# Transposed row maxima in the unused columns of the score banks, a third bank for products, a spread-out norm, Wo split during attention

## The chip, the cores and the metric

One NeuronCore of a Trainium2 chip runs the whole kernel. The metric is the device time of one execution in microseconds (us), the median of a few runs. In the profile the engines are PE (matrix multiply), PEld (its weight loads), DVE (vector), ACT (scalar), POOL (GpSimd) and SP (which issues most DMAs). PSUM, where PE writes its results, has eight banks of 2 KB per partition.

## The reference

Four layers on x of 2048 rows by 640 columns: a Fourier layer, an attention layer, and both again with the same weights.

```python
x = A_x
x = x + _A_ref(_layernorm(x), dft_seq_re, dft_seq_im, dft_hid_re, dft_hid_im)
x = x + _B_ref(_layernorm(x), wqkv, wo)
# ... and the same two lines once more
# _A_ref: a = x @ hid_re.T; b = x @ hid_im.T; y = seq_re @ a - seq_im @ b
# _B_ref: 32 heads of width 20, window 256 (key j is seen by query i where 0 <= i-j < 256):
#   scores = q @ k.T * 20**-0.5; p = softmax(masked scores); out = (p @ v) @ wo
```

## The kernel before

Every product of two fp32 matrices is made of fp16 halves (high and low part), so each 128x128 block costs three matmuls. `spectral(layer, ...)` is a Fourier layer and `attention(layer, ...)` an attention layer; they run as spectral 0, attention 0, spectral 1, attention 1.

**Order.** In the spectral layers a scheduler sets each engine's order at build time from priorities; generators in the list `side` advance one step at each `tick()`, of which there are seven per inner round `j`. In attention (`in_turn[0]` is true) each PE instruction is tied behind the one before it, so PE's order is the order in which the code issues it. All engines work strictly in the order of their own streams.

**Attention.** Rows are taken in 8 blocks `b` of 256, heads in 16 pairs; a step `g` handles one tile of 128 rows for one pair of heads, 256 steps per layer. In step `g` stand, in this order: `scores(g)` (four matmuls into the PSUM tile `sp` of two banks, of whose 512 columns per bank 384 are used; then DVE masks with COPY_PREDICATED, L1025, and takes the row maxima `m` with TENSOR_REDUCE, L1029); `by_key(g-7)` (the same scores transposed, tile `tp`, which need the maxima; ACT makes probabilities of them, L1068); every fourth step `values` and `back` (probabilities times v); then `run_fill`, which adds as many matmuls of other work as the step has time for. That other work (projections of the next block, output products, transpositions) is written to the PSUM tile `pf`, one bank each, from a pool of two; `new_f()` gives the next. It is emptied by ACT and DVE (`early`, L327 and L328; `x`, L869).

Every fourth step ends with `hand_on(n)`, which hands the maxima of four steps to `by_key`: ACT and DVE split them into `tops` (L1035, L1036), PE transposes `tops` in four matmuls into the tile `hp` (a bank of its own, pool `ph`), and two copies bring the result into rows of the query stack `qs`: ACT the rows of the first head (L1047), DVE those of the second (L1045, which waits for ACT's). `scores(g+1)` is what PE has next behind it. In the first block `qs` is a tile named `ks` in the profile.

PSUM's eight banks in attention: `pf` 2, `sp` 2, `tp` 2, `pv` 1, `hp` 1.

**The last round of a spectral layer.** From round `j` = 1 on, `finish(0)` and then `finish(1)` read the first four finished row tiles back from DRAM (`x2d`), normalise them on DVE (`norm_steps`, tiles `lnst`, `lnt`, `lny`), split them (`xs`) and transpose them on PE into `early`. `finish`'s second argument `pace` says how many norm steps go into one tick: 2 for the first call, 1 for the second.

**Wo.** In spectral 0, `b_split(0, 20)` scales and splits the weights of attention: 15 chunks of wqkv go back to DRAM (`bwd`), 5 chunks of wo stay in SBUF (`bo`), one chunk per five ticks. In attention, `slow_step()` advances the first generator of the list `slow` by one step per `g`.

Of the kernel before, what the change touches and what calls it, by code (L numbers as in the profile page):

```python
# [11 lines left out]
F32 = mybir.dt.float32  # L12
F16 = mybir.dt.float16
I32 = mybir.dt.int32
AF = mybir.ActivationFunctionType
OP = mybir.AluOpType
AX = mybir.AxisListType

S, D, H, DH, P = 2048, 640, 32, 20, 128
NT = S // P  # L20
ND = D // P
# [17 lines left out]
NEXT_STEPS = (10, 22)  # L39
# [19 lines left out]
def body(ctx: ExitStack, tc: tile.TileContext, x_in, cmat, whid, wqkv, wo, out):  # L59
    nc = tc.nc  # L60
# [45 lines left out]
    in_turn, latest = [False], [None]  # L106
# [72 lines left out]
    def new_f():  # L179
        return pf_.tile([P, 512], F32, tag="f", name="pf", bufs=2)  # L180
# [112 lines left out]
    class Projections:  # L293


        def __init__(self):
            n = 3 * ND * D
            big = new_big()
            self.w = [big[:, k * n:(k + 1) * n].rearrange("p (a b) -> p a b", a=ND) for k in range(2)]
            load_behind([(big[:, k * n:(k + 1) * n], bw_d[k].rearrange("p a b -> p (a b)")) for k in range(2)])  # L300
            self.rows = {}
            self.turn = 0
            self.stack = {}

        def new_rows(self, b):
            t = new_early()
# [3 lines left out]
            self.rows[b] = (x, [st[:, k] for k in range(NST)])  # L310

        def qk(self, b, w, ct):
            pf = new_f()
            cols = slice(w * D + ct * P, w * D + (ct + 1) * P)
            xt, stores = self.rows[b]
            k = 0
            for dt in range(ND):
                for l, r in ((0, 0), (0, 1), (1, 0)):
                    matmul(pf[:, :QB], self.w[l][:, dt, cols], xt[:, :, r, dt, :],
                                     start=k == 0, stop=k == 14)  # L320
                    k += 1
                    if k < 15:
                        yield 109
            t = stores[self.turn % len(stores)]
            self.turn += 1
            down = 8.0 / (X_UP * W_UP)
            nc.scalar.activation(t[:, 0], pf[:, :QB], AF.Copy, scale=down)  # L327
            nc.vector.scalar_tensor_tensor(t[:, 1], pf[:, :QB], down, t[:, 0], op0=OP.mult, op1=OP.subtract)  # L328
            load(qk_d[b][w].rearrange("a (c p) t -> c p a t", p=P)[ct], t)
            yield 109  # L330
# [5 lines left out]
    def spectral(layer, res_src, hidden, first):  # L336
        with ExitStack() as st:
# [204 lines left out]
            def main_c(r, j):  # L542
                res, cc, y, zb = state.pop((r, j))
                x0, x1 = res
                z = product(r, zb, cc, 6, False, True)
                add(x0[:, hi], z, x0[:, hi])
                tick()
                z = product(r, y, cc, 5, False, True)
                add(x1[:, lo], z, x1[:, lo])
                last = r == NR - 1  # L550
                for k in range(2):
                    nc.scalar.dma_start((x2_d if last else acc_d)[2 * j + k], res[k])
                if last and j == 0:
                    side.append(chain(finish(0, 2), finish(1, 1)))
                tick()

            def ahead(proj):
# [11 lines left out]
            def finish(j, pace):  # L569
                xs = [sb.tile([P, D], F32, tag="xin", name="x2", bufs=NXIN) for k in range(2)]  # L570
                for k in range(2):
                    load(xs[k], x2_d[2 * j + k])
                yield 1
                ys, xss = [], []
                for k, _ in enumerate(norm_steps(xs, ys)):
                    if k % pace == 0:
                        yield 1
                for y in ys:
                    xs = keep.tile([P, 2, D], F16, tag="xs", name="xs", bufs=2)
                    split(xs[:, 0], xs[:, 1], y, nc.gpsimd)  # L580
                    xss.append(xs)
                    yield 1
                proj.new_rows(j)
                for k, xs in enumerate(xss):
                    for m in range(2):
                        transposed(xs, m, proj.rows[j][0][:, k])
                        yield 1
                    finished[0] += 1
# [51 lines left out]
            def b_split(n0, n1):  # L640
                fs = {n: b_chunk(n) for n in range(n0, n0 + 3)}
                for _ in range(4):
                    yield 1
                for n in range(n0, n1):
                    f = fs.pop(n)
                    if n < 15:
                        t = keep.tile([P, 2, D], F16, tag="xto", name="bst", bufs=2)
                        hi, lo, sc = t[:, 0], t[:, 1], wsc[:, 0:1]
                    else:
                        hi, lo, sc = bo[0][:, n - 15], bo[1][:, n - 15], wsc[:, 1:2]  # L650
                    nc.scalar.activation(hi, f, AF.Copy, scale=sc)
                    yield 1
                    nc.vector.scalar_tensor_tensor(lo, f, sc, hi, op0=OP.mult, op1=OP.subtract)
                    if n < 15:
                        cs = slice((n % 3) * D, (n % 3 + 1) * D)
                        for k in range(2):
                            nc.scalar.dma_start(bw_d[k][:, n // 3, cs], t[:, k])
                    if n + 3 < n1:
                        fs[n + 3] = b_chunk(n + 3)
                    for _ in range(4):  # L660
                        yield 1

            def keep_w():
# [22 lines left out]
            for r in range(NR):  # L686
# [22 lines left out]
                for j in range(NJ):  # L709
                    n = r * NJ + j  # L710
                    if first:
                        if (r, j) == (0, 1):
                            side.append(chain(keep_w(), b_max()))
                        if (r, j) == (1, 0):
                            side.append(chain(b_scale(), b_split(0, 20)))
                    if r == NR - 1 and j == 3:
                        early_qk = ahead(proj)
                        side.append(early_qk)
# [41 lines left out]
    def attention(layer, proj, dst, final):  # L760
        with ExitStack() as st:
# [3 lines left out]
            def banks(name):  # L765
                return pool(name, space=bass.MemoryType.PSUM)
# [5 lines left out]
            else:  # L772
                pv_ = banks("pv")
                ps = banks("ps")
            ph = banks("ph")

            in_turn[0] = True
            VS_ = {}
# [115 lines left out]
            def next_norm(i, x3):  # L894
# [6 lines left out]
                if i < NT - 1:  # L901
                    fill.extend(Unit(now[0] + TURN_STEPS, g, "turn", now[0], [], True) for g in live[-1])

            def rows_norm(b, x2s):

                ys = []
                yield from norm_steps(x2s, ys)
                for t, y in enumerate(ys):
                    xs = new_xs()
                    split(xs[:, 0], xs[:, 1], y, nc.gpsimd)  # L910
                    live[-1].extend(rows_turn(b, xs, t, k) for k in range(2))
                    fill.extend(Unit(now[0] + TURN_STEPS // 2, g, ("rows", b), now[0], [], True) for g in live[-1])
                    yield
# [86 lines left out]

            TOP, PT, topped = {}, {}, [None]

            def place(g):

                b, r = divmod(g, 2 * NP)
                return 2 * b + r // 2 % 2, 2 * (r // 4) + r % 2

            def scores(g):
# [1 line left out]
                b = i // 2  # L1010
                qs = QS[b]
                t0 = (i % 2) * P
                sp = ps.tile([P, 2, 512], F32, tag="s", name="sp")
                if i % 2 == 0:
                    parts = [(0, 2 * P, b - 1, 0), (2 * P, 3 * P, b, 0)]
                else:
# [14 lines left out]
            def hand_on(n):  # L1031

                b, q = divmod(n, NP // 2)
                m, hl = TOP.pop(n), tops[n % 2]
                nc.scalar.activation(hl[:, :, :, 0], m, AF.Copy, scale=-1.0 / M_UP)  # L1035
                nc.vector.scalar_tensor_tensor(hl[:, :, :, 1], m, -1.0 / M_UP, hl[:, :, :, 0], op0=OP.mult, op1=OP.subtract)  # L1036
                hp = ph.tile([P, 4, P], F16, name="hp")
                for k in range(4):
                    transpose(hp[:66, k], hl[:, k].rearrange("p a b -> p (a b)")[:, :66], idh)
                for pi in range(2):  # L1040
                    rs = slice(64 * pi, 64 * pi + 2)
                    o = QS[b][rs, 2 * q:2 * q + 2].rearrange("r p (i t) -> r i p t", i=2)
                    t = hp[rs].rearrange("r (i p) t -> r i p t", i=2)
                    if pi:
                        nc.vector.tensor_copy(o, t)  # L1045
                    else:
                        nc.scalar.activation(o, t, AF.Copy)  # L1047
# [117 lines left out]
            total = NBQ * 60 * 136 + (NBQ - 1) * (150 * 109 + 60 * 136 + (4 if final else 8) * ND * 56)  # L1165
            total += 0 if final else 120 * 136
            total += (NBQ - 2) * 4 * ND * 56 - FIRST_FILL
            for g in range(NS):
                now[0] = g
                b, r = divmod(g, 2 * NP)  # L1170
# [10 lines left out]
                if g < NG and r == VALUE_LAG:  # L1181
# [7 lines left out]
                    if b == NBQ - 1 and not final:  # L1189
                        hidden = Hidden(xu_d)  # L1190
                        hidden.load()
                        for k in range(2):
                            hidden.fetch(k)
                            fill.append(Unit(g + NEXT_STEPS[k], hidden.stage(k, None), "next", NG + k))
                slow_step()
                n, m = divmod(g - VALUE_LAG, 4)
                if m == 0 and 0 <= n < NG // 4:
# [54 lines left out]
```

## Time and profile before

| | |
|---|---|
| median of 3 runs | 2322.34 us (2322.32 to 2322.77) |
| profiled execution, time | 2325.37 us |
| profiled execution, span from first to last instruction | 2323.6 us |
| busy, share of the span | PE 92%, DVE 75%, ACT 52%, POOL 52% |
| mean granted TensorE clock | 0.982 of full speed |
| first scores of attention 0 | 607.2 us |
| last scores of the kernel | 2293.9 us |

Busy PE is the sum of its matmuls' durations; what is left of 100% is time in which no matmul ran. A row of the waits says which instruction of an engine waited for which of another: total us, number of waits, longest. In the order of a program below, `[waits X_49]` names the engine whose count of finished instructions the instruction waits for, not the instruction.

### The profile page before, as it was taken

What the parts mean: (1) busy time and instruction counts of PE and PEld (TensorE: products, weight loads), DVE (VectorE), ACT (ScalarE), POOL (GpSimd) and SP (SyncE); (2) the same over time, 40 slices, a digit from 0 to 9 for tenths busy, and PEclk for the clock granted to TensorE, in tenths of its full rate; (3) what the DMA queues carried; (4) which work ended last, traced back from release to release, by engine and by line L of the source; (5) the groups of instructions that cost most, each with busy time, mean ns of one, the idle gap of its engine ahead of it and who ended that gap; (6) DMA issues with size and microseconds to landing.
All of it is one profiled execution on the core that took longest, in us unless ns stands there. A gap on an engine that the chain in (4) does not pass through costs nothing.

```text
span 2323.6 us, 54624 instructions
## 1 busy us (share of the span) xinstructions
PE 2143.3 (92%) x21985; PEld 1503.6 (65%) x21985; DVE 1746.8 (75%) x3761; ACT 1210.8 (52%) x2120; POOL 1199.3 (52%) x1453
## 2 busy tenths in 40 slices
PE   7999899989898999999889999999898989999997
PEld 5667566657566666666556777777665666666664
DVE  7887969767678788887767857584768777777674
ACT  5334444333266666676654344334325666666665
POOL 6776757655234444443347868584552334434343
PEclk9999999999999999999999999999999999999999
DMA  5864746454332332233324535464542322232120
GB/s 185 293 208 150 244 151 203 138 209 136 105 86 51 99 86 72 61 93 88 139 88 146 199 124 186 139 204 158 187 145 71 87 58 66 70 93 72 51 77 24
DMA packets 187602, 292.92 MB, mean 126 GB/s; under 512 B 13908, under 2 KB 120660, under 8 KB 178004
## 3 DMA queue, kind: packets, MB, share of 16 engines
q1 hardware_dynamic: 157108, 223.55, 31.7%
q10 hardware_dynamic: 30240, 65.88, 7.6%
q8 instruction: 172, 2.82, 0.5%
q14 instruction: 82, 0.67, 0.1%
HBM read 202.51 MB, written 86.87 MB: 125 GB/s over the span
## 4 chain that ended last, share of the span: by engine, by line
PE 63%; DVE 25%; DMA 5%; issue 3%; ACT 3%; POOL 1%; SPq 0%; DVEq 0%; ACTq 0%; POOLq 0%
PE pf L112 22%; PE y L112 11%; PE z L112 7%; PE x L112 7%; PE pv L112 7%; DVE m L1029 6%; PE sp L112 4%; DVE sp L1025 4%; DVE cc L480 4%; PE tp L112 2%; DVE qs L1045 1%; DMA x<-x2d 1%; DVE lnst L125 1%; DVE early L328 1%; DMA x2d<-res 1%
## 5 line engine op out<-in xcount | busy, mean ns | idle before, releaser
L112 PEld LDWEIGHTS <-cc 128*128 128x128 f16 x5376 | 530.5, 99 | 244.4 <-issue 33.1
L1068 ACT ACTIVATE ptq<-tp,shift,alpha 128x768 f32<-128x768 f32 (+2 forms) x512 | 484.4, 946 | 190.0 <-PE tp L112 145.9
L112 PEld LDWEIGHTS <-big 128*128 128x128 f16 x4320 | 409.1, 98 | 141.9 <-issue 32.1
L1073 POOL TENSOR_SCALAR_AFFINE_SELECT ptq<-ptq 128x512 f32<-128x512 f32 x224 | 144.2, 644 | 507.3 <-ACT ptq L1068 506.9
L1029 DVE TENSOR_REDUCE m<-sp 128x2 f32<-128x512 f32 (+1 forms) x512 | 344.9, 674 | 15.6
L112 PE MATMUL pf<-early,big 128*128 128x256 f16 x2400 | 310.1, 274 | 1.5 <-DVE early L328 1.4
L1025 DVE COPY_PREDICATED sp<-mask,sp 128x256 f32<-128x256 int32 x448 | 190.6, 425 | 129.1 <-PE sp L112 118.8
L112 PE MATMUL y<-zc,cc 128*128 128x320 f16 x1728 | 269.9, 304 | 16.0 <-DVE pf L503 16.0
L477 ACT ACTIVATE cc<-cs 128x512 f16<-128x512 f32 x256 | 152.3, 623 | 250.3 <-POOL cs L470 104.6
L112 PE MATMUL pf<-big 128*128 128x320 f16 x1680 | 241.9, 302 | 11.0 <-DVE zc L250 5.1
L480 DVE SCALAR_TENSOR_TENSOR cc<-cs,cc 128x512 f16<-128x512 f32 x256 | 231.4, 921 | 3.6 <-ACT cc L477 3.6
L1075 POOL TENSOR_SCALAR_AFFINE_SELECT ptq<-ptq 128x512 f32<-128x512 f32 x256 | 164.9, 644 | 94.4 <-ACT ptq L1068 94.4
L480 DVE SCALAR_TENSOR_TENSOR cc<-cq,cc 128x512 f16<-128x512 f32 x192 | 202.1, 1053 | 0.0
L112 PE MATMUL sp<-ks,qs 62*128 62x256 f16 (+1 forms) x1792 | 154.2, 249 | 45.0 <-DVE m L1029 39.8
L112 PE MATMUL pv<-ptq,v 128*32 128x128 f32 (+1 forms) x3840 | 186.9, 334 | 0.0
L112 PE MATMUL z<-zc,cc 128*128 128x320 f16 x1152 | 181.0, 302 | 4.2 <-DVE res L503 4.0
L112 PE MATMUL x<-zc,cc 128*128 128x320 f16 x1152 | 182.0, 302 | 0.0
L112 PE MATMUL pf<-big,early 128*128 128x320 f16 x960 | 158.3, 301 | 0.4 <-DVE early L927 0.4
L112 PE MATMUL tp<-qs,ks 62*128 62x128 f16 x2688 | 150.8, 217 | 3.2 <-ACT ptq L1068 2.9
L112 PE MATMUL pf<-bo,ot 128*128 128x320 f16 x840 | 145.6, 303 | 3.0 <-DVE x L869 1.1
L112 PEld LDWEIGHTS pv<-ptq,v 128*32 128x32 f32 x3840 | 108.3, 111 | 57.7 <-issue 4.0
L112 PEld LDWEIGHTS <-ks 62*128 62x128 f16 x3008 | 116.0, 95 | 39.8 <-DVE m L1029 23.2
(142 smaller groups left out, 3382.6 us busy)
## 6 DMA issues: line engine op xcount, KB each, us to landing
cq<-in_cmat_dram SPq DMA_DIRECT2D x64, 1024.0 KB
accd<-res ACTq DMA_DIRECT2D x96, 320.0 KB
res<-accd SPq DMA_DIRECT2D x96, 320.0 KB
x<-x2d SPq DMA_DIRECT2D x64, 320.0 KB
qkd<-early SPq DMA_DIRECT2D x160, 128.0 KB
ks<-qkd SPq DMA_DIRECT2D x108, 160.0 KB
qs<-qkd SPq DMA_DIRECT2D x84, 160.0 KB
x2d<-res ACTq DMA_DIRECT2D x32, 320.0 KB
```

What stands on the lines that cost most here:

```text
L112: i = getattr(nc.tensor, what)(*args, **kw)
L125: nc.vector.bn_stats(st[:, h], x[:, h * 320:(h + 1) * 320])
L328: nc.vector.scalar_tensor_tensor(t[:, 1], pf[:, :QB], down, t[:, 0], op0=OP.mult, op1=OP.subtract)
L477: nc.scalar.activation(cc[m][:, 0], f, AF.Copy, scale=C_UP)
L480: nc.vector.scalar_tensor_tensor(cc[m][:, 1], f, C_UP, cc[m][:, 0], op0=OP.mult, op1=OP.subtract)
L1025: nc.vector.copy_predicated(sp[:, :, 2 * P:3 * P], mask[:, None, :].to_broadcast([P, 2, P]), far)
L1029: topped[0] = nc.vector.tensor_reduce(TOP[g // 4][:, g % 4], sp[:, :, c0:3 * P], axis=AX.X, op=OP.max).ins
L1045: nc.vector.tensor_copy(o, t)
L1068: nc.scalar.activation(q[:, h:h + 2, a0 + first:a0 + 3], tp[:, :, first * P:3 * P].rearrange("p a (b c) -> p a b c", c=P), AF.Sigmoid, bia ...
L1073: nc.gpsimd.affine_select(out=q[:, :, a0], in_=q[:, :, a0], pattern=[[0, 4], [-1, P]], base=0, channel_multiplier=1, compare_op=OP.is_gt, ...
L1075: ins = nc.gpsimd.affine_select(out=q[:, :, a0 + 2], in_=q[:, :, a0 + 2], pattern=[[0, 4], [1, P]], base=0, channel_multiplier=-1, compare ...
```

## The change

1. The tile `sp` is made once per attention layer and not once per step, and the bank of `hp` is given up: PE's four transpositions go into columns 384 to 511 of the two `sp` banks, which the scores leave unused (`hp[0]`, `hp[1]`), and the two copies read from there.
2. The bank that is free becomes the pool `p3`: in attention every third `new_f()` comes from it, so `pf` products rotate over three banks.
3. `finish` yields three times behind its loads (one before), and every norm step has its own tick in both calls (`pace` 1, and `pace` now counts ticks per step).
4. `b_split` ends at chunk 15 and takes six ticks per chunk. `split_wo()` does the five chunks of wo as the first generator of `slow` in attention 0: it loads them on SP's queue into `res` buffers and splits one per step on ACT and DVE.

```diff
@@ class Projections
+            self.new_f = new_f
...
-            pf = new_f()
+            pf = self.new_f()
@@ spectral
-                    side.append(chain(finish(0, 2), finish(1, 1)))
+                    side.append(chain(finish(0, 1), finish(1, 1)))
...
-                yield 1
+                for _ in range(3):
+                    yield 1
                 ys, xss = [], []
-                for k, _ in enumerate(norm_steps(xs, ys)):
-                    if k % pace == 0:
+                for _ in norm_steps(xs, ys):
+                    for _ in range(pace):
                         yield 1
...
-                            side.append(chain(b_scale(), b_split(0, 20)))
+                            side.append(chain(b_scale(), b_split(0, 15)))
@@ attention
-            ph = banks("ph")
+            p3 = banks("p3")
+            third = [0]
+
+            def new_f():
+                third[0] += 1
+                if third[0] % 3 or not in_turn[0]:
+                    return pf_.tile([P, 512], F32, tag="f", name="pf", bufs=2)
+                return p3.tile([P, 512], F32, tag="f", name="pf")
+
+            proj.new_f = new_f
...
+            def split_wo():
+                fs = [keep.tile([P, D], F32, tag="res", name="wst", bufs=4) for n in range(2)]
+                for n in range(2):
+                    load(fs[n], wo[:, n])
+                yield
+                for n in range(ND):
+                    f, sc = fs.pop(0), wsc[:, 1:2]
+                    nc.scalar.activation(bo[0][:, n], f, AF.Copy, scale=sc)
+                    nc.vector.scalar_tensor_tensor(bo[1][:, n], f, sc, bo[0][:, n], op0=OP.mult, op1=OP.subtract)
+                    if n + 2 < ND:
+                        fs.append(keep.tile([P, D], F32, tag="res", name="wst", bufs=4))
+                        load(fs[-1], wo[:, n + 2])
+                    yield
...
+            sp = ps.tile([P, 2, 512], F32, tag="s", name="sp")
+            hp = [sp[:, k, 3 * P:].bitcast(F16).rearrange("p (a b) -> p a b", a=2) for k in range(2)]
...
             def scores(g):
-                sp = ps.tile([P, 2, 512], F32, tag="s", name="sp")
...
             def hand_on(n):
-                hp = ph.tile([P, 4, P], F16, name="hp")
                 for k in range(4):
-                    transpose(hp[:66, k], hl[:, k].rearrange("p a b -> p (a b)")[:, :66], idh)
+                    transpose(hp[k // 2][:66, k % 2], hl[:, k].rearrange("p a b -> p (a b)")[:, :66], idh)
                 for pi in range(2):
                     rs = slice(64 * pi, 64 * pi + 2)
                     o = QS[b][rs, 2 * q:2 * q + 2].rearrange("r p (i t) -> r i p t", i=2)
-                    t = hp[rs].rearrange("r (i p) t -> r i p t", i=2)
+                    t = sp[rs, :, 3 * P:].bitcast(F16).rearrange("r i (p t) -> r i p t", p=2)
...
+            if layer == 0:
+                slow.append(split_wo())
```

What the programs' orders say, at three places.

PE at a hand-over (`hand_on`, then the next `scores`; here `tops_77` is the buffer with the split maxima), before:

```order
L112 MATMUL hp<-idh,tops_77 66x128
L112 LDWEIGHTS tops_77
L112 MATMUL hp<-idh,tops_77 66x128
L112 LDWEIGHTS qs [waits DVE_49]
L112 MATMUL sp<-ks,qs 128x128 [waits PE_49]
L112 LDWEIGHTS qs
L112 MATMUL sp<-ks,qs 128x128
```

and after the change:

```order
L112 LDWEIGHTS tops_77
L112 MATMUL sp<-idh,tops_77 66x128 [waits DVE_49]
L112 LDWEIGHTS tops_77
L112 MATMUL sp<-idh,tops_77 66x128
L112 LDWEIGHTS qs
L112 MATMUL sp<-ks,qs 128x128 [waits DVE_49]
L112 LDWEIGHTS qs
L112 MATMUL sp<-ks,qs 128x128
```

No instruction moved, but the waits did. Before, the weight load ahead of the next scores waited for a DVE count that is reached with the row maxima of the step before (L1029). Now the first score matmul waits for a DVE count that is reached with the DVE copy out of the same banks (L1069, before L1045), in all 126 hand-overs that have scores behind them (63 in each layer); and the first transposition waits for the last row maxima taken from `sp`.

DVE around that copy (in the same hand-over's neighbourhood, attention 0), before:

```order
L1025 COPY_PREDICATED sp<-mask,sp 128x2x128 [waits DVE_49,PE_49]
L1029 TENSOR_REDUCE m<-sp 128x2 [waits DVE_49]
L1045 COPY qs<-hp 2x2x2x128 [waits Activation_49]
L1116 RECIPROCAL r<-pv 128x8 [waits PE_49]
L1117 TENSOR_TENSOR o<-pv,r 128x160 [waits DVE_49,Pool_49]
```

and after the change:

```order
L950 COPY xto<-pf 128x640 [waits PE_49]
L1069 COPY qs<-sp 2x2x2x128 [waits Activation_49]
L1050 COPY_PREDICATED sp<-mask,sp 128x2x128 [waits DVE_49,PE_49]
L1054 TENSOR_REDUCE m<-sp 128x2 [waits DVE_49]
L1140 RECIPROCAL r<-pv 128x8 [waits PE_49]
```

The copy of the maxima, which stood behind the mask of the next scores (and here behind their maxima too), now stands ahead of it.

DVE in the last round of spectral 0, where `finish(0)` ends (`lny` are the two normalised tiles, `lnt` the last norm steps, `cc` splits of the Fourier matrix, `pf<-y` and `res<-z` the sums that empty PE's banks), before:

```order
L142 TENSOR_TENSOR lnt<-lnt 128x2 [waits DVE_49]
L143 SCALAR_TENSOR_TENSOR lnt<-lnt 128x2 [waits DVE_49]
L147 TENSOR_SCALAR lny<-x_5744,lnmv,lnt 128x640 [waits DVE_49]
L147 TENSOR_SCALAR lny<-x_5745,lnmv,lnt 128x640
L503 SCALAR_TENSOR_TENSOR pf<-y,pf 128x320 [waits PE_49]
L480 SCALAR_TENSOR_TENSOR cc<-cs,cc 128x512 [waits Activation_49] x2
L390 COPY early<-pf 128x640 [waits PE_49] x2
```

and after the change:

```order
L143 SCALAR_TENSOR_TENSOR lnt<-lnt 128x2 [waits DVE_49]
L504 SCALAR_TENSOR_TENSOR pf<-y,pf 128x320 [waits PE_49]
L481 SCALAR_TENSOR_TENSOR cc<-cs,cc 128x512 [waits Activation_49]
L147 TENSOR_SCALAR lny<-x_5724,lnmv,lnt 128x640 [waits DVE_49]
L481 SCALAR_TENSOR_TENSOR cc<-cs,cc 128x512 [waits Activation_49]
L147 TENSOR_SCALAR lny<-x_5725,lnmv,lnt 128x640
L504 SCALAR_TENSOR_TENSOR res<-z,res 128x320 [waits PE_49,Pool_49]
```

The sum `pf<-y` now stands ahead of the normalised tiles, and on PE the first transposition of them stands 40 matmuls later than before (58 in spectral 1).

More of the change, by code (lines that the diff above doesn't have):

```diff
@@ L645, in b_split @@
                     f = fs.pop(n)
[L646 to L650, printed above, removed]
+                    t = keep.tile([P, 2, D], F16, tag="xto", name="bst", bufs=2)
+                    hi, lo, sc = t[:, 0], t[:, 1], wsc[:, 0:1]
                     nc.scalar.activation(hi, f, AF.Copy, scale=sc)
@@ L653, in b_split @@
                     nc.vector.scalar_tensor_tensor(lo, f, sc, hi, op0=OP.mult, op1=OP.subtract)
[L654 to L657, printed above, removed]
+                    cs = slice((n % 3) * D, (n % 3 + 1) * D)
+                    for k in range(2):
+                        nc.scalar.dma_start(bw_d[k][:, n // 3, cs], t[:, k])
                     if n + 3 < n1:
                         fs[n + 3] = b_chunk(n + 3)
-                    for _ in range(4):
+                    for _ in range(5):
                         yield 1
@@ L1193, in attention @@
                             hidden.fetch(k)
-                            fill.append(Unit(g + NEXT_STEPS[k], hidden.stage(k, None), "next", NG + k))
+                            fill.append(Unit(g + NEXT_STEPS[k], hidden.stage(k, None, new_f), "next", NG + k))
                 slow_step()
```

## The prediction

> **What bounds the kernel now.** I read first the busy time by stage (spectral 0, attention 0, spectral 1, attention 1; columns: window, its length, busy time of each engine, clock, DMA share, GB/s), then PE's waits, then single hand-overs in the timeline.
>
> ```profile
> core 0: us, PE busy (x) PEld busy (x) DVE busy (x) ACT busy (x) POOL busy (x), PEclk, DMA share, GB/s
> 0.00:607.00 607.00, 551.32 (x4014) 391.89 (x4015) 474.68 (x881) 248.06 (x482) 385.71 (x326) 0.97 0.57 190
> 607.00:1243.00 636.00, 580.44 (x7421) 400.03 (x7421) 499.50 (x1302) 409.86 (x676) 263.22 (x450) 0.99 0.29 84
> 1243.00:1738.00 495.00, 482.35 (x3573) 348.99 (x3571) 346.72 (x551) 184.48 (x370) 333.42 (x272) 0.99 0.51 171
> 1738.00:2323.60 585.60, 529.15 (x6979) 362.74 (x6978) 425.90 (x1029) 368.45 (x594) 216.90 (x412) 0.99 0.25 68
> ```
>
> PE is the bound everywhere: 580.4 of 636.0 us and 529.2 of 585.6 us in the two attentions. So all the time that better waits can give back there is 55.6 + 56.4 = 112 us, and any new wait of PE is added to the span. PE's longest waits over the whole span (total us, times, longest):
>
> ```profile
> PE sp L112 <- DVE m L1029: 49.9, 91, 1.8
> PE y L112 <- DVE pf L503: 25.0, 11, 5.3
> PE pf L112 <- DVE early L328: 19.6, 25, 1.6
> PE pf L112 <- DVE x L869: 12.5, 14, 4.2
> ```
>
> The first is PE waiting for the row maxima before it may overwrite `sp`; the last two are products waiting for one of the two `pf` banks. Now a hand-over in the middle of attention 0 (start, duration):
>
> ```profile
> 907.50 0.39 PE L112 MATMUL hp<-idh,tops 128*66 128x128 f16 x4
> 907.82 0.34 PE L112 MATMUL sp<-ks,qs 62*128 62x128 f16 x4
> 907.92 0.59 ACT L1047 ACTIVATE qs<-hp 2x512 f16<-2x512 f16 x1 [0.37 <-PE hp L112]
> 908.20 0.43 DVE L1025 COPY_PREDICATED sp<-mask,sp 128x256 f32<-128x256 int32 x1
> 908.66 0.42 DVE L1045 COPY qs<-hp 2x512 f16<-2x512 f16 x1
> ```
>
> PE goes from the transpositions (modelled end 907.89) straight into the next scores at 907.82, 0.07 us before that end, while ACT and DVE only begin to copy. The copies end at 909.08 and nobody on PE waits for them. That is what the change takes away.
>
> **The hand-over, step by step.** In the changed program the first score matmul behind the transpositions waits for the DVE copy. Nothing of PE's work stands between them, so PE idles from the end of the transpositions to the end of that copy. What the copy needs, in the last hand-over of the kernel, where nothing stood in its way:
>
> ```profile
> 2298.44 0.39 PE L112 MATMUL hp<-idh,tops 128*66 128x128 f16 x4
> 2298.86 0.59 ACT L1047 ACTIVATE qs<-hp 2x512 f16<-2x512 f16 x1
> 2299.48 0.42 DVE L1045 COPY qs<-hp 2x512 f16<-2x512 f16 x1 [3.36 <-ACT qs L1047]
> ```
>
> ACT starts 0.03 us behind the transpositions' end (2298.83), DVE 0.03 us behind ACT's end (2299.45), and the copy ends at 2299.90, 1.07 us behind the transpositions. From the end of a DVE instruction to PE's start it takes 0.05 us, in the wait of 2.93 us at the end of spectral 0:
>
> ```profile
> 509.03 0.48 DVE L503 SCALAR_TENSOR_TENSOR pf<-y,pf 128x320 f32<-128x320 f32 x1
> 509.56 1.79 PE L112 MATMUL y<-zc,cc 128*128 128x320 f16 x12 [2.93 <-DVE pf L503]
> 511.19 1.25 PE L112 MATMUL x<-zc,cc 128*128 128x320 f16 x8
> ```
>
> With the 0.07 us of overlap that is lost, the floor of a hand-over is 1.07 + 0.05 + 0.07 = 1.19 us. A late one, where DVE was busy with a norm:
>
> ```profile
> 1969.93 0.39 PE L112 MATMUL hp<-idh,tops 128*66 128x128 f16 x4
> 1971.48 0.41 DVE L1025 COPY_PREDICATED sp<-mask,sp 128x256 f32<-128x256 int32 x1
> 1971.92 0.42 DVE L1045 COPY qs<-hp 2x512 f16<-2x512 f16 x1
> ```
>
> Here the copy ends 2.02 us behind the transpositions, so 2.14 us in all; 0.41 us of it is the mask, which the new order puts behind the copy. How many are late, from the rows of the tile `hp` (minimum/median/maximum in ns; then the idle time that the transpositions ended):
>
> ```profile
> L1047 ACT ACTIVATE qs<-hp x112: 570/587/587, 678.2 to 2298.9; 2x512 f16<-2x512 f16 x112
> L1045 DVE COPY qs<-hp x112: 422/422/424, 678.9 to 2299.5; 2x512 f16<-2x512 f16 x112
>   PE hp L112: 56.8, 77
> ```
>
> The two copies' durations hardly vary, and in 77 of 128 hand-overs ACT sat idle for the transpositions. I take the floor for those and 0.4 us more for the other 51, nearer the floor than the late one, since the mask's 0.41 us is gone: 1.19 + 51/128 x 0.4 = 1.35 us. With scores behind it a hand-over occurs 63 times in each attention: 126 x 1.35 = **+170 us**, bounds 126 x 1.19 = 150 and 126 x 2.14 = 270. Queued behind the waiting matmul are the other scores, `by_key`'s matmuls and so ACT's probabilities; they come as much later as PE does, and DVE, in its copy, stands ahead of the next mask and maxima, so it cannot work ahead either.
>
> By the rows alone one could hope that the wait is a formality, since matmuls and copies ran side by side at 907.92 without harm, in different banks: the price would be 0. [...]
>
> **What comes back.** (a) Waits for the maxima, 49.9 us: a hand-over stands before every fourth step's scores, and its wait takes the place of about a quarter, 12; of the other 37 I take a quarter, 9, since DVE is given 1.2 us in every four steps to catch up: **-21 us** (0 to -50). (b) The third bank: 19.6 + 12.5 = 32.1 us of waits for two banks; three give a product one more product's time, over a microsecond against waits of 0.8 us on average: **-27 us** (0 to -32). (c) The spread norm. The waits around `finish` in spectral 0 (500 to 525 us) and spectral 1 (1640 to 1655 us):
>
> ```profile
> PE pf L112 <- ACT xs L159: 5.3, 1, 5.3
> PE y L112 <- DVE pf L503: 2.9, 1, 2.9
> PE pf L112 <- POOL xs L160: 1.1, 1, 1.1
> ...
> PE y L112 <- DVE pf L503: 5.3, 1, 5.3
> PE pf L112 <- ACT xs L159: 3.6, 1, 3.6
> PE pf L112 <- POOL xs L160: 0.4, 1, 0.4
> ```
>
> They sum to 18.6 us. The norm takes DVE as long as before, but PE now has 40 and 58 matmuls more to do before it needs the result, at 12 in 1.63 us (509.56 to 511.19) 5.4 and 7.9 us: at most 13.3 us come back, I take **-12 us** (0 to -19).
>
> **What is moved at no cost.** Wo's five splits leave spectral 0 for the first steps of attention 0:
>
> ```profile
> L112 PE MATMUL pf<-bo,ot x840: 296/299/474, 704.8 to 2300.8; 128*128 128x320 f16 x168
> L651 ACT ACTIVATE bo<-wst,wsc x5: 812/817/819, 352.9 to 384.0; 128x640 f16<-128x640 f32 x5
> L653 DVE SCALAR_TENSOR_TENSOR bo<-wst,wsc,bo x5: 871/1479/1883, 357.8 to 396.8; 128x640 f16<-128x640 f32 x5
> ```
>
> That is about 5 x 1.48 us of DVE and 5 x 0.82 us of ACT, from a stage where DVE is 78% busy into one where it is 79% busy: 0, and 5 x 1.48 = 7.4 us either way if neither stage covers it. The first product that reads `bo` runs at 704.8 us, 97 us behind the start of attention 0, so the five loads on SP's queue (DMA share 0.29 there), ahead of which stand only the first stacks' loads, have time; the next block's loads come behind them. The weight load ahead of the scores no longer waits itself; it takes less than the copies' wait and hides in it: 0. `b_split`'s wider spacing ends before the last round, where its result is loaded: 0.
>
> **The clock.** New idle time could lower the granted clock. Four stretches of 3.4 us, two by two in sequence (columns as in the first view):
>
> ```profile
> 661.90:665.30 3.40, 1.47 (x18) 0.93 (x16) 2.98 (x7) 2.24 (x5) 1.56 (x3) 1.00 0.00 0
> 665.30:668.70 3.40, 3.40 (x33) 1.56 (x32) 1.32 (x4) 0.97 (x3) 0.64 (x1) 0.50 0.02 5
> 712.00:715.40 3.40, 2.15 (x22) 1.48 (x23) 3.24 (x14) 1.46 (x2) 1.23 (x2) 1.00 0.04 14
> 715.70:719.10 3.40, 2.14 (x28) 1.39 (x29) 2.98 (x8) 2.54 (x4) 1.83 (x3) 1.00 0.25 96
> ```
>
> After a stretch with 1.47 us of PE work the clock was 0.50 for the next; after one with 2.15 us it stayed at 1.00. A hand-over alone leaves 3.4 - 1.35 = 2.05 us of work, just on the safe side; a second wait beside it is not. A half-clock stretch costs up to 3.4/2 = 1.7 us: I take three, **+5 us**, and 126/3 = 42 of them, 71 us, as the far end.
> [...]
>
> **Sum.** 170 - 21 - 27 - 12 + 5 = +115 us on the span of 2323.6, so 2438.6 us. The profiled execution took 2325.37 us, 3.0 above the median of 2322.34; against that median the sum is 2322.3 + 115 = **2437 us**, with own bounds of 2395 to 2495.
>
> **Rivals.** *The waits absorb it.* DVE's backlog is the cause of most waits, and PE's pauses clear it: hand-overs at their floor, 150, and all of 49.9 + 32.1 + 18.6 = 100.6 us back: +49, **2372 us**. For it: all three groups wait for DVE or ACT. Against: in its copy DVE is held back too. *The clock swings:* 71 us in place of 5, **2503 us**; the same place is reached by late hand-overs at 1.9 us each. For it: 2.05 us is close to 1.47. *The wait is over in time* (the other side): the copy is done before PE reaches the scores, and (b) and (c) remain: 2322 - 39 = **2283 us**. It decides from the point where a hand-over costs less than (21 + 27 + 12)/126 = 0.48 us; against it, the copies alone last 0.59 + 0.42 = 1.01 us, one behind the other, in all of the trace's hand-overs shown, with no other work of PE between. *The spread norm and the third bank do nothing:* +154, 2476, inside the range.
>
> **Chances.** Forecast 0.70; absorbed (2330 to 2395) 0.16; clock or late hand-overs (above 2495) 0.09; in time 0.04; and 0.01 for no change within 0.2%, about what a measurement of this kernel can tell. So slower 0.95, same 0.01, faster 0.04. The range leaves out the last two and the upper end of the third: 2380 to 2500 us.
>
> **What would show it.** In the changed profile: a row "PE sp <- DVE qs" (the copy) with about 126 waits and 150 to 180 us; PE's transpositions named `sp<-idh,tops`; `sp <- m` below 35 us; `pf <- early` and `pf <- x` below 10 us together; the waits around `finish` near 6 us; attention 0 near 690 us and attention 1 near 640; clock above 0.97. I am wrong if that row is missing or its waits average under half a microsecond, or if the clock falls below 0.95 in attention.

## The result and the profile after

The changed kernel takes 2446.49 us (2445.51 to 2447.54), 1.0534 times the kernel before, with a 95% interval of 1.0516 to 1.0552. It is slower by about 124 us; 115 had been forecast. Its profiled execution has a span of 2445.8 us, 122 us above the 2323.6 of before, and the account below is made of these two spans. The times of the experiments are compared as ratios to the kernel before on the same chip.

The stages again, cut at the same places of the program (columns as in the prediction's first view; last line the sum):

```profile
0.00:602.00 602.00, 547.22 (x4016) 390.03 (x4016) 473.66 (x876) 246.25 (x479) 385.68 (x333) 0.98 0.56 190
602.00:1300.00 698.00, 584.36 (x7410) 412.44 (x7411) 505.90 (x1306) 418.27 (x679) 263.53 (x442) 0.97 0.27 78
1300.00:1792.00 492.00, 483.85 (x3586) 349.68 (x3583) 347.77 (x551) 184.53 (x370) 333.78 (x280) 0.99 0.51 172
1792.00:2445.80 653.80, 539.97 (x6978) 378.40 (x6978) 430.28 (x1028) 375.05 (x593) 215.84 (x400) 0.97 0.22 60
sum 2445.80, PE 2155.41 PEld 1530.55 DVE 1757.60 ACT 1224.10 POOL 1198.82; mean PE 538.85 PEld 382.64 DVE 439.40 ACT 306.02 POOL 299.71
```

All of the loss is in the two attentions: 636.0 to 698.0 us and 585.6 to 653.8 us, together +130; the spectral layers became 5 and 3 us shorter. PE is busy 2155.4 us in place of 2143.3, so of the 122 us some 12 are busy time and 110 are idle time. (Busy PE in these tables is the time in which at least one matmul ran, not the sum of the matmuls' durations: matmuls that overlap count once, and an overlap that is lost adds to it.) Which idle time, from PE's waits in the changed kernel:

```profile
PE sp L112 <- DVE qs L1069: 136.9, 110, 2.8
PE sp L112 <- DVE m L1054: 37.9, 63, 1.7
...
PE sp L112 <- DVE ks L1069: 20.2, 16, 2.1
...
PE pf L112 <- DVE x L877: 5.9, 7, 1.7
...
PE pf L112 <- DVE early L329: 2.3, 3, 0.9
```

The first and the third row did not exist before: 110 + 16 = 126 waits of the scores for the copy of the transposed maxima, 157.1 us, 1.25 us each. The rows that the third bank was for fell from 32.1 to 8.2 us. One hand-over in the middle of attention 0, engine by engine:

```profile
986.27 0.39 PE L112 MATMUL sp<-idh,tops 128*66 128x128 f16 x4
986.69 0.59 ACT L1071 ACTIVATE qs<-sp 2x512 f16<-2x512 f16 x1 [0.36 <-PE sp L112]
987.31 0.42 DVE L1069 COPY qs<-sp 2x512 f16<-2x512 f16 x1 [0.81 <-ACT qs L1071]
987.79 0.34 PE L112 MATMUL sp<-ks,qs 62*128 62x128 f16 x4 [1.13 <-DVE qs L1069]
```

The reader should see a chain with one link per engine and no gap over 0.06 us in it: transpositions to 986.66, ACT to 987.28, DVE to 987.73, PE at 987.79. PE waits 1.13 us, which is the median of the 126 waits (the least is 1.13, the longest 2.84). Before, PE's next scores began 0.07 us ahead of the end of that chain's first link. That overlap is lost too: the four transpositions and the four scores took 0.66 us of PE together at 907.50 before, and take 0.39 + 0.34 = 0.73 us here. In 126 hand-overs (0.066 us each in the mean) this is some 8 us, which stand in PE's busy time and not in the waits.

### The profile page after: what moved, and what is told of

The parts are those of the page before. It is cut to its first block, busy times and chain, and to the rows that moved or that the text cites. A ratio compares the mean times of both kernels' runs of the same rounds, so it can differ in the third digit from the quotient of the medians.

```text
span 2445.8 us, 54756 instructions
## 1 busy us (share of the span) xinstructions
PE 2155.4 (88%) x21985; PEld 1530.6 (63%) x21985; DVE 1757.6 (72%) x3761; ACT 1224.1 (50%) x2120; POOL 1198.8 (49%) x1453
## 4 chain that ended last, share of the span: by engine, by line
PE 62%; DVE 22%; ACT 6%; DMA 5%; issue 4%; POOL 1%; SPq 0%; ACTq 0%; DVEq 0%; POOLq 0%
PE pf L112 25%; PE y L112 9%; PE pv L112 7%; PE sp L112 6%; PE x L112 6%; PE z L112 6%; DVE cc L481 4%; DVE m L1054 4%; PE tp L112 2%; ACT qs L1071 2%; DVE sp L1050 2%; DVE qs L1069 2%; DVE res L504 1%; ACT ptq L1092 1%; DVE lny L147 1%
## 5 line engine op out<-in xcount | busy, mean ns | idle before, releaser
L112 PEld LDWEIGHTS <-qs 62*128 62x128 f16 x1792 | 66.7, 94 | 240.7 <-issue 225.1
L112 PE MATMUL pf<-big,early 128*128 128x320 f16 x960 | 164.7, 309 | 0.0
L112 PEld LDWEIGHTS <-ks 62*128 62x128 f16 x3008 | 124.7, 96 | 49.0 <-issue 42.3
```

The costliest lines, as they stand in the source:

```text
L112: i = getattr(nc.tensor, what)(*args, **kw)
```

## The experiments

**The maxima out of the score banks.** Here they take a turn in the three product banks; everything else is as in the changed kernel.

```diff
-            hp = [sp[:, k, 3 * P:].bitcast(F16)... for k in range(2)]
@@ hand_on
+                hp = new_f().bitcast(F16)[:, :4 * P].rearrange("p (a b) -> p a b", a=4)
```

> The changed kernel, but the transposed maxima take a turn in the three product banks (a whole bank for about 1.1 us) and leave the score banks alone. Theory (the loss is PE's wait for the copies out of the score banks, 157 us in 126 waits): that row vanishes, and with the other gains kept the time is below the kernel before, 2285 to 2310 us. Rival 1 (PE waits for the copies wherever they are, since by_key needs them, or the maxima hold up the product that comes two turns later): a new wait of 0.5 us or more per hand-over, 2350 us or above. Rival 2 (the loss is in the other parts: Wo in attention, the spread norm, the lower clock): 2420 us or above.

Measured: ratio 1.0006 (0.9994 to 1.0019). Its longest waits of PE, and a short one:

```profile
PE sp L112 <- DVE m L1053: 46.8, 88, 1.8
PE pf L112 <- DVE early L329: 26.9, 28, 2.1
PE y L112 <- DVE pf L504: 25.4, 11, 4.2
PE pf L112 <- DVE x L877: 16.6, 16, 3.9
...
PE pf L112 <- DVE qs L1069: 1.8, 4, 0.8
```

No row of scores waiting for a copy is left, and the 5.3% are gone. That settles where the loss was; rival 2 (the other parts) fell. It was not `sp` being made once per layer either, since that is kept here. But the time was expected below 2310 us and is not below the kernel before: the waits for product banks are 43.5 us, more than the 32.1 with two banks, which takes back the 10 us that the norm and Wo give (next experiment). Of these waits 6 us are the transpositions themselves waiting for a bank, and 27 us come 2 to 5 us behind them (18 us before). This fits rival 1's second half, that the maxima hold a bank which products then miss, at a smaller price than it named; only the last row, 1.8 us, names the copy, so it is not shown wait by wait.

**The spread norm and Wo's split, without the new banks.**

```diff
+                hp = ph.tile([P, 4, P], F16, name="hp")
...
@@ new_f
-                if third[0] % 3 or not in_turn[0]:
+                if True:
...
@@ scores
+                sp = ps.tile([P, 2, 512], F32, tag="s", name="sp")
```

> The kernel before with only the spread norm and the Wo split during attention (maxima in their own bank, two product banks). Theory: the waits around the norm fall from 18.6 us to about 13 as in the changed kernel, Wo costs nothing: 2312 to 2320 us. Rival (Wo's splits delay the first steps of attention 0 or the larger wait of 6.8 us at the end of attention 0 comes from here): 2323 to 2335 us.

Measured: ratio 0.9955 (0.9940 to 0.9971), 10 us faster than before; the rival (2323 us or more) fell. So these two parts gain, and the loss is in the banks: sharing the score banks costs 149 us by itself (1.0594 in the next experiment against 0.9955), and 135 us together with the third bank (1.0534).

**The sharing without the third bank.**

```diff
@@ new_f
-                if third[0] % 3 or not in_turn[0]:
+                if True:
-                return p3.tile([P, 512], F32, tag="f", name="pf")
```

> The changed kernel without the third product bank (the bank stays empty). Theory (the third bank took 24 us of waits for products away): these waits come back in part, since PE's pauses at the hand-overs give DVE time to empty the banks: 2455 to 2472 us. Rival (the pauses alone empty the banks in time, the third bank is worth nothing now): 2444 to 2449 us.

Measured: ratio 1.0594 (1.0559 to 1.0629), 14 us above the changed kernel and within the theory's range. Its waits:

```profile
PE sp L112 <- DVE qs L1067: 137.4, 110, 3.0
PE sp L112 <- DVE m L1052: 35.9, 61, 1.6
...
PE sp L112 <- DVE ks L1067: 19.8, 16, 1.7
PE pf L112 <- DVE early L329: 11.1, 19, 1.1
...
PE pf L112 <- DVE x L875: 7.4, 12, 2.2
```

The hand-over costs the same 157.2 us whether there is a third bank or not. Without it the waits for product banks are 18.5 us, against 8.2 with it and 32.1 in the kernel before: PE's pauses had already removed 14 of the 24 us that had been booked to the third bank, and the bank itself removed 10.

The third bank also has a price that no term of the forecast names. At the end of attention 0 the changed kernel has this wait (620 to 1310 us):

```profile
PE pf L112 <- ACT xs L159: 6.8, 1, 6.8
```

PE stands at the first transposition of the next layer's rows (`xs`) until ACT has split them. The same wait is 6.4 to 6.8 us in all four kernels of this study whose third bank is for products alone, and 0.9 to 1.9 us in the six others. What makes PE arrive so early, or ACT so late, was not traced.

**Both copies on DVE**, which replaces a link of 0.59 us by one of 0.42.

```diff
-                    if pi:
-                        nc.vector.tensor_copy(o, t)
-                    else:
-                        nc.scalar.activation(o, t, AF.Copy)
+                    nc.vector.tensor_copy(o, t)
```

> The changed kernel with both copies of the transposed maxima on DVE: the 0.59 us of ACT is replaced by 0.42 us of DVE. Theory (PE waits for exactly this chain of two copies): each of the 126 waits is 0.15 to 0.2 us shorter, 19 to 25 us in all, 2420 to 2430 us. Rival (the wait is set by DVE being late, so that more work on DVE lengthens it): same or slower, 2445 to 2470 us.

Measured: ratio 1.0421 (1.0391 to 1.0451), about 26 us faster than the changed kernel. The two rows of the wait are

```profile
PE sp L112 <- DVE qs L1068: 118.7, 110, 2.5
...
PE sp L112 <- DVE ks L1068: 16.9, 16, 1.9
```

135.6 us in 126 waits, with a median of 0.94 us: 0.19 us less than 1.13, which is about ACT's 0.59 less 0.42 and one start of an engine (0.03 us in the hand-over at 986.27 above, from ACT's end at 987.28 to DVE's start at 987.31). The wait follows the length of the chain, and the theory's numbers hold.

**Cover between the transpositions and the scores.**

```diff
-                run_fill(max(rate, 400) * FILL[(g - VALUE_LAG + 2) % 4])
+                amount = max(rate, 400) * FILL[(g - VALUE_LAG + 2) % 4]
...
-                if m == 0 and 0 <= n < NG // 4:
+                handing = m == 0 and 0 <= n < NG // 4
+                run_fill(amount / 2 if handing else amount)
+                if handing:
                     hand_on(n)
+                    run_fill(amount / 2)
```

> The changed kernel with half of the step's other matmuls (about 7, some 0.9 us) moved from ahead of the hand-over to between the transpositions and the next scores. Theory (PE waits because it has nothing else to do while the copies run): the 126 waits of 1.25 us fall to about 0.4 us, 157 us to 50 us; the transpositions come earlier and may wait for the row maxima, 10 to 30 us in all: 2350 to 2380 us. Rival (the copies are late because DVE and ACT are busy, and cover does not help): above 2420 us.

Measured: ratio 1.0362 (1.0340 to 1.0384), 40 us faster than the changed kernel, half of what was expected. First its waits, then one hand-over on PE:

```profile
PE sp L112 <- DVE m L1054: 78.3, 149, 3.1
PE sp L112 <- DVE qs L1069: 63.9, 103, 2.3
...
PE sp L112 <- DVE ks L1069: 8.3, 16, 0.9
```

```profile
980.38 0.38 PE L112 MATMUL sp<-idh,tops 128*66 128x128 f16 x4 [0.30 <-DVE lnt L132]
980.61 0.84 PE L112 MATMUL pf<-big,early 128*128 128x320 f16 x5
981.90 0.34 PE L112 MATMUL sp<-ks,qs 62*128 62x128 f16 x4 [0.45 <-DVE qs L1069]
```

The wait for the copies fell from 157 to 72 us, as the cover of 0.84 us leaves 0.45. But the waits for the maxima grew from 37.9 to 78.3 us: the transpositions also write into the score banks, and come so early now that DVE still reads the last scores there (the 0.30 us in the first row; the instruction it names is DVE's next one behind the maxima). In 105 of the 128 hand-overs the transpositions now wait more than 0.15 us, 54 us in all; in the changed kernel it was 22, and 15 us. Sharing the banks made two waits here, and the work that was put ahead of one of them uncovered the other.

**The maxima in a bank that is free at that time**: the upper half of `pv`, which otherwise only `back` uses. `back` runs one step later than before.

```diff
-BACK_LAG = 14
+BACK_LAG = 15
@@ hand_on
...
+                hp = pv[:, 2:].bitcast(F16).rearrange("p a (b c) -> p (a b) c", c=P)
```

> The changed kernel, but the transposed maxima lie in the upper half of the bank pv, which is free between two uses by back(), and back() runs one step later; the third product bank stays. Theory: no hand-over wait on PE (its next use of that bank is over two microseconds away), the product waits stay near 8 us as in the changed kernel, the norm's gain stays: 2285 to 2305 us, faster than the kernel before and than the norm and Wo alone (2316 us). Rival (the third bank's gain was only a by-product of PE's pauses, or back() one step later holds up the output products): 2312 to 2330 us.

Measured: ratio 0.9932 (0.9914 to 0.9951), the fastest of all, 16 us below the kernel before. Lines of its waits:

```profile
PE sp L112 <- DVE m L1053: 45.9, 95, 2.1
...
PE pf L112 <- DVE x L877: 12.4, 9, 5.1
...
PE pv L112 <- DVE o L1138: 6.2, 13, 1.0
...
PE pf L112 <- DVE early L329: 2.6, 4, 0.8
```

There is no hand-over wait, and the product waits are 15.0 us in place of 32.1. Still the result misses what was expected: 0.9932 of 2322.3 is 2306.5 us, just above the upper end of 2305 and some 11 us above the middle. The product waits are 7 us above the changed kernel's. The first matmuls of `values`, which follow one step behind `back` now and not two, wait 12 us in all for `pv` (6.2 of them in the row shown), and never did before. The wait for `xs` at the end of attention 0 is 6.4 us here. In the profiled executions 12 of the 17 us by which the span is shorter are busy time, with the granted clock at 0.988 in place of 0.982, and only 5 are idle time. Against norm and Wo alone (0.9955) the third bank is worth some 5 us here, which the two intervals do not quite separate.

**The norm alone, and Wo alone**, each on the kernel before, with the lines of the change's third and fourth part.

```diff
-                    side.append(chain(finish(0, 2), finish(1, 1)))
+                    side.append(chain(finish(0, 1), finish(1, 1)))
```

> The kernel before with only the spread norm. Theory: it brings the 6 us by which the waits around the norm fell in the changed kernel, and the clock there a little more: 2313 to 2318 us. Rival (the gain of 10 us of norm and Wo together is Wo's): 2319 to 2323 us.

```diff
-                            side.append(chain(b_scale(), b_split(0, 20)))
+                            side.append(chain(b_scale(), b_split(0, 15)))
@@ attention
+            if layer == 0:
+                slow.append(split_wo())
```

> The kernel before with only the Wo split during attention. Theory (covered in both stages): 2318 to 2325 us. Rival (Wo's leaving spectral 0 is the gain of 10 us): 2311 to 2317 us.

Measured: norm 0.9963 (0.9949 to 0.9977), 9 us faster; Wo 0.9978 (0.9966 to 0.9991), 5 us faster. The norm's gain, to 2313.7 us, is the theory's. In its profile PE's waits in the last rounds of the two spectral layers fall from 23.8 to 12.9 us, but its profiled execution (2325.74 us) was the slowest of the eleven and its span shows no gain. Wo's gain is small, though its interval leaves out 1, and its 2317.2 us lie between the two expectations. Its profiled execution (2332.92 us) was the slowest of twelve and shows no row in which these 5 us could be read, so where they come from is open.

## Why the prediction was right, by its own steps

- **The hand-over: +170 forecast, about 165 measured:** 157.1 us of waits and some 8 us of lost overlap, which the step had in its floor of 1.19 us. The mechanism was as described and shown by two doses (0.19 us less per wait, or 0.84 us of cover) and by its removal. Without the overlap the floor was 1.12 us, and the median wait is 1.13. The late hand-overs were mis-sized: 27 of 126 waits are above 1.2 us, not the 51 of 128 taken from ACT's idle times, but they are late by 0.5 us in the mean and not 0.4.
- **Waits for the maxima: -21 forecast, -12 measured** (49.9 to 37.9). The quarter that the hand-over's wait replaces is about all; DVE did not catch up further.
- **Third bank: -27 forecast, -24 measured**, but only 10 of them belong to the bank by the experiment with two banks. The step gave the whole to the bank and left the pauses out.
- **The norm: -12 forecast, about -8.** In the last rounds (495 to 602 us, then 1640 to 1792 us) the changed kernel waits:

```profile
PE y L112 <- DVE pf L504: 2.9, 2, 2.3
PE pf L112 <- ACT early L393: 2.7, 1, 2.7
PE z L112 <- DVE res L504: 1.4, 2, 0.8
PE pf L112 <- POOL xs L160: 1.2, 1, 1.2
...
PE y L112 <- DVE pf L504: 4.7, 2, 4.1
PE pf L112 <- POOL xs L160: 1.2, 1, 1.2
PE pf L112 <- ACT early L393: 0.8, 1, 0.8
...
PE z L112 <- DVE res L504: 0.6, 1, 0.6
```

  These are 15.5 us, some 12 of them around `finish`. Before, the same rounds had 23.8 us: the 18.6 of the prediction's rows and 5.2 us of `z` (2.3 and 1.7) and `y` (0.6 twice). The waits for ACT's split of the normalised rows (`xs`, 5.3 and 3.6) are gone, as forecast; those for POOL's split and for sums that still stand behind norm steps on DVE remain, and 3.5 us for `early` are new; the step's count of matmuls did not contain them. Over the whole spectral layers PE's idle time, length less busy time in the stage tables, fell only from 55.7 to 54.8 and from 12.7 to 8.2 us.
- **The clock: +5 forecast, about +4.** PE's busy time grew by 12 us with the same number of matmuls, and some 8 of them are the lost overlap. One of the stretches at half clock, and the 3.4 us ahead of it:

```profile
717.50:720.90 3.40, 1.19 (x10) 0.78 (x9) 2.62 (x9) 1.55 (x4) 0.35 (x1) 1.00 0.00 0
720.90:724.30 3.40, 2.85 (x19) 1.82 (x19) 2.23 (x6) 1.66 (x3) 3.33 (x4) 0.50 0.00 0
```

  A late hand-over (a wait of 1.84 us that ends at 721.45) and a wait of its transpositions for the maxima (0.92 us) left 1.19 us of work in 3.4, and the next stretch ran at half clock. The clock records of the trace have 24 spells of half clock in place of 17; in the changed kernel each began behind 3.41 us with at most 1.85 us of PE work, and the 2.05 us that a hand-over alone leaves lie above all 24, as the step had it. The far end of 71 us, with such a stretch in every third hand-over, was the author's estimate; the traces show 24 - 17 = 7 spells more. That the 4 us are the hand-overs' is not shown: PE's busy time lies between 2131 and 2150 us in the other kernels without shared score banks.
- **Wo: 0 forecast, about -5 alone**, within the 7.4 us allowed either way.

The sum of the measured terms, 157 + 8 - 12 - 24 - 8 + 4 = 125 us, is near the 122 us by which the span grew; other rows of a few us each, in both directions, make up the difference, the wait of 6.8 us at the end of attention 0 among them. The three terms that were to give time back came to 44 us and not 60, which the forecast of 115 lacks, and the hand-over cost 5 us less than forecast, which hides a part of that. Two signs that the prediction named were missed: `sp <- m` was to fall below 35 us and is 37.9, and the waits around `finish` were to be near 6 us and are about twice that. The rival in which the waits absorb the hand-overs fell because only 44 of the 100 us named there came back (12 on `sp`, 24 on `pf`, 8 in the last rounds), and the one in which the copies are done in time because nothing on PE stands between. The hopeful reading of the rows, by which the price would be 0, was wrong: the wait was there in all 126 places, 1.25 us in the mean. It is the program's own; no run here shows what the chip does without it.

## What to carry to other kernels

Free columns in a bank were not free here: the scores waited for copies out of columns that they do not write, so a small tile put into another tile's bank joined both tiles' chains, and PE stood still for two copies of 0.59 and 0.42 us, 126 times. (Whether the program keeps this wait by bank or by tile these runs do not tell apart, since the maxima lay inside the tile `sp`.) Ask which bank is idle at that time, not which has room; the upper half of `pv` took the same data without a wait of the scores, at the price of 12 us of waits for `pv`. And count what an engine has to do, in the order of its program, between a write and the next use of its bank: here it was nothing, and every link of the chain was paid in full (1.13 us in the median wait); with 0.84 us of other work between, the wait shown was 0.45 us.

## What the runs showed of the hardware that was not expected

Pauses of PE took away nearly as many waits for product banks as a third bank did: 32.1 us became 18.5 with pauses and two banks, and 15.0 with three banks and no pauses at the hand-over. And the granted clock went to half after a stretch with 1.19 us of matmuls in 3.4 us, in an attention whose mean load on PE was 84% (584.4 of 698.0 us). PE need not be idle for that: the busiest such stretch of the changed kernel, the 3.41 us ahead of 2379.8, had 1.85 us of work (54%), and the clock granted in the next was 0.50.
